# A spectral filter and a SwiGLU block on one core: idle products, a pipeline distance and the places of preparation in the first batch

## The chip, the core and the metric

The kernel runs on one core of a Trainium2 chip. The core has five engines with a queue each: TensorE (PE; its weight loads are listed apart as PEld), VectorE (DVE), ScalarE (ACT), GpSimd (POOL) and SyncE (SP), which in this kernel issues most of the DMAs. The metric is device time in microseconds, from the first to the last instruction of one launch and what lies around them; less is better. The time before is the median of five runs.

## The reference

There are two parts. The first filters x along the sequence in the frequency domain; the second is a SwiGLU block with weights given in float64.

```python
batch, seq, dim = (8, 3008, 256);  d_ff = 1536
X = np.fft.rfft(x, axis=1)
F = (filt_r + 1j * filt_i)[None, :, :]
y = np.fft.irfft(X * F, n=x.shape[1], axis=1).astype(np.float32)
x = y.reshape(B * S, D)                       # 24064 tokens of 256
g = x @ w_gate                                # 256 x 1536
silu = g * (1.0 / (1.0 + np.exp(-g)))
val = x @ w_val                               # 256 x 1536
out = (silu * val @ w_out).astype(np.float32) # 1536 x 256
```

## The kernel before

**The filter** of one batch is a Fourier transform in steps, 3008 = 47 x 64. Stage 1 multiplies x with a small table (`stage1_first` in the first batch, tiles `wpa`; `stage1` later, tiles `pa`). The middle steps, twelve of them (`u` from 0 to 11), are: `turn` (transposes, `wpt`), `stage2a` (a product with a table, `wpb`, then products with the filter on DVE and their sum on POOL) and `stage2b` (the way back, `wpc`, a copy on ACT and a write to the DRAM tile `d`). Stage 3 reads that tile again and makes the filtered y of one chunk of 376 tokens (`wpd` for the first chunk, `pd` for the others). In the first batch all of this up to the first chunk stands at the front of the program, with nothing else to do; in later batches it is spread over the steps of the batch before.

**The SwiGLU block** works through 8 batches x 8 chunks x 3 groups of hidden columns. One such step (class `Group`) is a list of tokens, `SCHEDULE`, that fixes the order of all instructions by hand. Its products with the weights follow a scheme that saves products: 26 products of 128-wide pieces, in order `Q0 Q1 P3 P1 P0 A13 Q2 P2 A01 B13 B01 Q3 A02 A12 E12 B02 E02 B12 E13 A23 A03 E23 E01 B23 E03 B03`. `P` and `Q` take pieces of y (tile `y`, PSUM tile `wk`); `A`, `B` and `E` take sums of pieces (tile `y_t`, PSUM tiles `wa`, `we`) and sums of weights. The weights lie in `wt_t` in that same order, two slots of 128 columns to a product. `D` tokens are differences that POOL makes (tile `D`) before the products of a pair can go on; `S` tokens are sums of the hidden activations on POOL (`h`); `W` and `o` are the projection of the step before (`wA`, `wF`, `wG`, added to `o`); `t` tokens run pieces of the filter; `n` tokens make or reload the sums of the next chunk (`combine_sequence`, `reload_sums`).

**The order in the first batch.** Steps 0 to 8 take chunks 0, 1, 2 in group 0, then in group 1, then in group 2. So y of these chunks is kept in DRAM (`keep_y`) and read again (`reload_y`, L927 of the profile) for the next step; at step 8 it is y of chunk 3, whose sums are made right after. Such extra work hangs on a token of a step by `chore`.

**The weights' rounding.** The float64 weights are rounded on the core (`round_half`: four DVE, four ACT and one or more POOL instructions for each of 36 halves, L302 to L342), and sums of weights are made from them (`combine_weights`: a sum on DVE, for three of the six pairs a factor on ACT, two sums on POOL, L225 to L232). Class `Preparation` puts these on a line of ticks: half `i` begins 4 ticks after the one before, 8 where the first projection half (`i` = 8) begins. A tick issues its instructions in program order, where it stands. There are 8 ticks in stage 1, two in each middle step, and `finish(0)` runs those that the first step needs; after that `TICKS` ticks are spread over a step, and `finish(step)` runs the remaining ones that a step needs at its start.

**Idle products.** `idle(t, banks, n)` issues matmuls whose result nobody reads, one a PSUM bank. There are five at the start, two before the fifth and two before the seventh part of stage 1, 14 on finished weights ahead of stage 3 (`warm`), and three behind it. PE takes its matmuls in order. An fp32 matmul is two passes in the profile, so a count of x4 is two products.

The waits that the build writes into the program are semaphore counts on the writer of what is read. Buffers come from pools that rotate: seven PSUM banks of one pool carry all tiles whose name begins with `w`.

## Time and profile before

| | us |
|---|---|
| median of 5 runs | 2964.26 |
| lowest, highest | 2963.31, 2966.64 |
| the profiled execution's own time | 2966.64 |
| its span, first to last instruction | 2964.9 |
| PE busy | 2925.2 |
| DVE, ACT, POOL busy | 1931.8, 1610.5, 1584.8 |

The mean granted clock of the profiled execution is 0.996. The chain of waits that ended last is PE for 92% of the span, and no other engine has more than 1% of it. How full the engines are in the first batch's parts (busy us in the stretch, and the granted clock of PE):

| stretch, us | what | PE | DVE | ACT | POOL | clock |
|---|---|---|---|---|---|---|
| 8 to 28 | stage 1 | 19.41 | 7.77 | 8.99 | 0.00 | 1.00 |
| 28 to 72 | middle steps | 30.17 | 35.70 | 31.11 | 21.96 | 0.92 |
| 72 to 87 | sums of weights, stage 3 | 14.89 | 10.85 | 7.40 | 12.45 | 0.88 |
| 87 to 120 | step 0 | 26.56 | 25.70 | 23.40 | 24.22 | 0.90 |
| 120 to 200 | steps 1 to 3 | 76.11 | 68.67 | 58.04 | 71.26 | 1.00 |
| 200 to 340 | steps 3 to 7 | 136.40 | 113.05 | 83.37 | 78.29 | 1.00 |
| 340 to 373 | step 8 | 29.77 | 20.96 | 14.71 | 21.87 | 0.95 |

A busy PE in this table counts idle products too. In the lines that follow, the first number is the start from the span's begin, the second the length; in square brackets stands how long the engine had been idle before and what ended it. A line of the weights' or y's sums carries the line number of the helper (`add` L225, `sub` L228, `negated_sum` L232), so its tiles tell which it is.

### The profile page before, as it was taken

How to read it: one execution, taken by the hardware profiler on the slowest of the kernel's cores; microseconds unless marked ns; L12 is line 12 of the kernel's file. 1: busy time of each engine (PE TensorE's matmuls, PEld its weight loads, DVE VectorE, ACT ScalarE, POOL GpSimd, SP SyncE). 2: the span in 40 equal slices, each digit the busy share in tenths (PEclk: the TensorE clock that was granted, in tenths of full speed). 3: DMA queues.
4: the chain of work that ended last, by engine and by line, in shares of the span. 5: the costliest groups of instructions: out<-in, count | busy, mean ns of one | idle time of the engine just before them, and what ended most of it. 6: DMA issues, size and time to landing. Idle time of an engine off the chain costs nothing.

```text
span 2964.9 us, 57673 instructions
## 1 busy us (share of the span) xinstructions
PE 2925.2 (99%) x20292; PEld 2826.5 (95%) x20292; DVE 1931.8 (65%) x4379; ACT 1610.5 (54%) x4207; POOL 1584.8 (53%) x1764
## 2 busy tenths in 40 slices
PE   7999999999999999999999999999999999999999
PEld 5888999999999999999999999999999999999999
DVE  5888765576655766557765577656676566766665
ACT  5775455555555555554555554555555555555554
POOL 3776464455545464446554555544564545555453
PEclk9999999999999999999999999999999999999999
DMA  8577865566555755557555566465665566644442
GB/s 211 184 257 256 275 214 165 186 205 199 174 182 181 219 185 174 189 177 224 188 169 182 186 206 209 153 191 187 198 207 162 185 203 189 208 139 148 147 132 89
DMA packets 217081, 558.59 MB, mean 188 GB/s; under 512 B 29872, under 2 KB 107552, under 8 KB 216512
## 3 DMA queue, kind: packets, MB, share of 16 engines
q1 hardware_dynamic: 170954, 485.59, 52.1%
q10 hardware_dynamic: 36912, 45.43, 4.5%
q0 software_dynamic: 8928, 23.89, 2.3%
q8 instruction: 163, 2.67, 0.4%
q14 instruction: 124, 1.02, 0.1%
HBM read 459.73 MB, written 95.05 MB: 187 GB/s over the span
## 4 chain that ended last, share of the span: by engine, by line
PE 92%; DVE 1%; DMA 1%; POOL 1%; issue 0%; SPq 0%; ACT 0%; ACTq 0%
PE wa L731 24%; PE wA L810 17%; PE wk L731 16%; PE we L731 12%; PE wG L810 8%; PE wF L810 4%; PE pd L639 3%; PE pa L551 3%; PE pc L623 2%; PE pb L591 2%; DMA y<-y 0%; DMA lent<-in_filt_r_dram 0%; DMA lent<-de_tbl 0%; POOL wt_t L225 0%; POOL wt_t L228 0%
## 5 line engine op out<-in xcount | busy, mean ns | idle before, releaser
L731 PE MATMUL wa<-y_t,wt_t 128*128 128x188 f32 x4464 | 882.7, 324 | 9.6 <-DVE wa L753 2.9
L731 PEld LDWEIGHTS wa<-y_t,wt_t 128*128 128x128 f32 x4464 | 732.0, 191 | 35.1 <-issue 14.4
L225 POOL TENSOR_TENSOR h<-h 128x376 f32<-128x376 f32 x190 | 182.8, 983 | 793.9 <-DVE h L778 793.9
L810 PE MATMUL wA<-wo_t,h 128*128 128x128 f32 x4608 | 577.9, 275 | 3.8 <-DVE o L225 3.0
L810 PEld LDWEIGHTS wA<-wo_t,h 128*128 128x128 f32 x4608 | 562.9, 192 | 18.0 <-issue 11.2
L731 PE MATMUL wk<-y,wt_t 128*128 128x188 f32 x2976 | 568.0, 324 | 0.0
L228 POOL TENSOR_TENSOR h<-h 128x376 f32<-128x376 f32 x570 | 555.6, 996 | 0.5
L731 PEld LDWEIGHTS wk<-y,wt_t 128*128 128x128 f32 x2976 | 479.2, 191 | 25.9 <-issue 19.8
L228 DVE TENSOR_TENSOR we<-we,m 128x376 f32<-128x376 f32 x576 | 318.7, 556 | 198.4 <-PE we L731 140.6
L731 PE MATMUL we<-y_t,wt_t 128*128 128x188 f32 x2232 | 432.7, 323 | 0.6 <-ACT we L762 0.5
L731 PEld LDWEIGHTS we<-y_t,wt_t 128*128 128x128 f32 x2232 | 370.6, 190 | 1.4 <-ACT we L762 1.0
L228 POOL TENSOR_TENSOR D<-f,f 128x376 f32<-128x376 f32 x288 | 279.9, 985 | 104.7 <-ACT f L746 103.9
L232 DVE SCALAR_TENSOR_TENSOR y<-wk,c 128x376 f32<-128x376 f32 x480 | 245.1, 543 | 132.3 <-ACT we L762 82.6
L766 ACT COPY m<-wa 128x376 f32<-128x376 f32 x576 | 271.9, 472 | 88.7 <-PE wa L731 87.7
L773 ACT ACTIVATE g<-wa 128x188 f32<-128x188 f32 x576 | 187.9, 326 | 189.2 <-PE wa L731 181.6
L810 PE MATMUL wG<-wo_t,h 128*128 128x128 f32 x2304 | 288.3, 275 | 0.6 <-DVE o L225 0.6
L810 PEld LDWEIGHTS wG<-wo_t,h 128*128 128x128 f32 x2304 | 281.4, 192 | 0.8 <-DVE o L225 0.8
L773 ACT ACTIVATE u<-we 128x188 f32<-128x188 f32 x576 | 188.9, 328 | 167.4 <-DVE we L228 148.3
L746 ACT ACTIVATE f<-wk 128x376 f32<-128x376 f32 x288 | 139.2, 483 | 236.3 <-PE wk L731 213.6
L750 ACT COPY c<-wk 128x376 f32<-128x376 f32 x288 | 136.0, 472 | 226.7 <-PE wk L731 226.7
L753 DVE SCALAR_TENSOR_TENSOR x<-wk,f 128x376 f32<-128x376 f32 x192 | 104.6, 545 | 230.2 <-PE wk L731 228.9
L762 ACT COPY we<-y 128x376 f32<-128x376 f32 x480 | 223.8, 486 | 32.8 <-DVE h L778 14.2
(140 smaller groups left out, 3936.3 us busy)
## 6 DMA issues: line engine op xcount, KB each, us to landing
wt_t<-w_all SPq DMA_DIRECT2D x174, 896.0 KB
wt_t<-w_all SPq DMA_DIRECT2D x174, 768.0 KB
t<-d SPq DMA_DIRECT2D x62, 384.0 KB
d<-t ACTq DMA_DIRECT2D x112, 192.0 KB
lent<-de_tbl SPq DMA_DIRECT2D x84, 256.0 KB
lent<-in_filt_r_dram SPq DMA_DIRECT2D x336, 64.0 KB
lent<-d SPq DMA_DIRECT2D x84, 256.0 KB
d<-lent ACTq DMA_DIRECT2D x84, 256.0 KB
```

Source lines behind the costliest of these rows:

```text
L225: return eng.tensor_tensor(out=dst, in0=a, in1=b, op=ALU.add)
L228: return eng.tensor_tensor(out=dst, in0=a, in1=b, op=ALU.subtract)
L232: return nc.vector.scalar_tensor_tensor(out=dst, in0=a, scalar=-1.0, in1=b, op0=ALU.mult, op1=ALU.subtract)
L551: pin(nc.tensor.matmul(out=ps[0:NK], lhsT=wf_t, rhs=self.x.pop(u), start=True, stop=True))
L731: pin(nc.tensor.matmul(out=ps[:, z], lhsT=self.wt[:, SLOT[p], z], rhs=rhs, start=start and z == 0, stop=True, skip_group_check=True))
L746: pin(act.mul(self.small(f"f{i}", f"f{i}", 1), t[f"k{i}"], -1.0))
L750: pin(act.copy(out=self.small(f"c{i}", f"c{i}", 1), in_=t[f"k{i}"]))
L753: pin(v.scalar_tensor_tensor(out=dst, in0=t[f"k{j}"], scalar=-1.0, in1=t[f"f{i}" if j == 3 else f"D{at}"], op0=ALU.mult, op1=ALU.add))
L762: pin(act.copy(out=self.bank(f"e{at}"), in_=t[f"y{at}"]))
L766: pin(act.copy(out=self.small(f"m{at}", "m", 4), in_=t[f"a{at}"]))
L773: pin(act.activation(out=self.small(op, "g", 3, 1)[:, 0], in_=ps[:, 1], func=AF.Silu))
L810: pin(nc.tensor.matmul(out=self.tiles[at][:, t, :], lhsT=self.hs[i][:, HID[p], t0:t0 + 128], rhs=wo_t[:, JB * q + i, WO[p], :], start=star ...
```

## The change

Only the first batch changes. Stage 1 gets one or two idle products before each part but the first: ten in all, not four. The middle steps run `stage2b` four steps behind `stage2a`, not three. The 14 idle products of `warm` are replaced by eight, in four pairs; a pair reads the slot of a weights' sum (A13, A01, A02, A12) and, as its moving operand of 512 columns, that slot and the next one in the order of products. The first projection half begins 16 ticks after the one before it, not 8, and a step has 22 ticks, not 20. `reload_y` hangs on P0, the fifth product of a step, from step 3 on; at step 2 it stays at A02, the thirteenth.

```diff
@@ class Preparation
-                b = base[-1] + (4 if i != 2 * len(BLOCKS) else 8) if i else 0
+                b = base[-1] + (4 if i != 2 * len(BLOCKS) else 16) if i else 0
...
-    TICKS = 20
+    TICKS = 22
@@ idle products
-    def warm():
-
-        banks = [bank("idle") for _ in range(NB)]
-        for n in (TQ, 2 * TQ):
-            idle(wt_t[:, 0:2].rearrange("p s z f -> p (s z f)"), banks, n)
@@ the front of the first batch
         for u in range(8):
-            if u in (4, 6):
-                idle(zero, [bank("idle") for _ in range(2)], 512)
+            if u:
+                idle(zero, [bank("idle") for _ in range(2 - u % 2)], 512)
             spec.stage1_first(u)
...
-        lag = 3
+        lag = 4
...
         preparation.finish(0)
-        warm()
+        for p in ("A13", "A01", "A02", "A12"):
+            at = SLOT[p]
+            idle(wt_t[:, at:at + 2].rearrange("p s z f -> p (s z f)"),
+                 [bank("idle") for _ in range(2)], 512)
         for step in (0, 2, 1, 3):
             run(spec.stage3(0, step))
@@ chores
     for step in range(NT - 1, NT * NG):
-        chore(step, "A02", lambda s: reload_y(order_of(0)[s + 1][0], s), step)
+        chore(step, "A02" if step < NT else "P0", lambda s: reload_y(order_of(0)[s + 1][0], s), step)
```

## The prediction

> **What bounds the kernel now.** I read the page's busy shares first. TensorE (PE) is busy for 2925.2 of 2964.9 us, so no more than about 40 us can be won without removing products, and a stretch table says where they lie: nearly all before 373 us, in the first batch, which is the part that changes.

> ```profile
> PE 2925.2 (99%) x20292; PEld 2826.5 (95%) x20292; DVE 1931.8 (65%) x4379; ACT 1610.5 (54%) x4207; POOL 1584.8 (53%) x1764
> 28.00:72.00 44.00, 30.17 (x137) 22.47 (x135) 35.70 (x65) 31.11 (x63) 21.96 (x28) 0.92 0.85 212
> 87.00:120.00 33.00, 26.56 (x146) 24.24 (x144) 25.70 (x59) 23.40 (x66) 24.22 (x31) 0.90 0.45 143
> 373.00:2964.90 2591.90, 2585.38 (x18168) 2519.91 (x18166) 1648.49 (x3786) 1382.01 (x3624) 1354.58 (x1471) 1.00 0.57 182
> ```

> The columns after the length are busy us of PE, its weight loads, DVE, ACT, POOL, then granted clock, DMA share, GB/s. From 28 to 72 us (the middle steps) DVE is the fullest engine.

> Next the timeline of PE at the front, and DVE's waits between 29.9 and 72 us.

> ```profile
> 8.75 7.28 PE L564 MATMUL wpa<-wf_t,wo_t 94*128 94x96 f32 x64
> 15.87 1.91 PE L461 MATMUL widle<-room 128*128 128x512 f32 x4
> 17.62 3.71 PE L564 MATMUL wpa<-wf_t,y_t 94*128 94x96 f32 x32
> 27.02 0.33 PE L577 MATMUL wpt<-unit,lent 128*128 128x128 f32 x1 [0.40 <-ACT lent L568]
> DVE room L600 <- ACT y_t L616: 2.8, 5, 0.7
> DVE room L603 <- PE wpb L591: 1.9, 1, 1.9
> DVE w L302 <- POOL wt_t L228: 0.7, 2, 0.4
> ```

> Stage 1 runs on PE without a gap from 8.75 us: it waits for no load. In the middle steps DVE waits for PE once, at the start.

> Last, the timelines of 72 to 98 us and around 359 us.

> ```profile
> 72.11 2.08 PE L623 MATMUL wpc<-room,tb 128*128 128x256 f32 x4 [1.61 <-POOL room L225]
> 73.98 7.58 PE L461 MATMUL widle<-wt_t 128*128 128x188 f32 x28
> 81.40 3.71 PE L639 MATMUL wpd<-wi_t,f 96*128 96x94 f32 x32
> 84.94 2.77 PE L461 MATMUL widle<-room 128*128 128x512 f32 x6
> 84.50 0.77 POOL L225 TENSOR_TENSOR wt_t<-wt_t 128x256 f32<-128x256 f32 x1
> 88.22 0.73 POOL L225 TENSOR_TENSOR wt_t<-wt_t 128x256 f32<-128x256 f32 x1
> 96.41 0.97 POOL L228 TENSOR_TENSOR D<-f,f 128x376 f32<-128x376 f32 x1
> 98.04 1.22 PE L731 MATMUL wa<-y_t,wt_t 128*128 128x188 f32 x6 [2.94 <-DVE wa L753]
> 358.94 0.43 SPq L927 DMA_DIRECT2D y<-y  x1
> 367.46 0.92 ACT L682 ACTIVATE y_t<-y 128x376 f32<-128x376 f32 x2 [3.57 <-DMA y<-y]
> 369.02 1.60 PE L731 MATMUL wa<-y_t,wt_t 128*128 128x188 f32 x4 [2.04 <-ACT wa L757]
> ```

> After the last middle product PE idles on purpose for 7.6 us, then makes y (wpd). POOL has the weights' twelve sums until 88.95, y's sums until 96.4, and only then D01, for which PE stands 2.94 us.

> **1. Ten idle products in stage 1 instead of four: +5.25 us.** Two old ones hold PE from 15.87 to 17.62, so one costs 0.875 us; six more are 6 x 0.875 = 5.25. Nothing hides them. Stage 1 is on PE, the first transpose at 27.02 waits for the copy of its last bank, and DVE's chain starts from the transposes. They could be free only if x landed late, but SP's issue times (an issue is held until the eighth transfer before it has landed) show x in the core 1.2 to 1.7 us before PE wants it, even with the old idle products. Bounds 4.5 and 5.7 (0.955 each with pipeline ends).

> [...] Row: from 7.26 to 33.9 us the clock is at 1.00 throughout, and it fell in windows where PE was busy little, as in 65.29 to 68.70 (1.21 of 3.41 us, no gap over 2.2). So stage 1 has no half clock to win back. [...]

> **2. Distance of four: 0.** PE gets to a wpc one step later and waits less there (its waits on wpc are 9.3 us in all), but DVE's waits in these steps are for ACT's copies L616 and POOL, never for PE after the first. The tail ends, as now, with the sum of step 11 on POOL (72.06) and one wpc. Bounds: -1.0 (this wpc at full clock, 1.10 for 2.08) and +1.1 (one more of ACT's copies with its DMA issue in the tail). I take 0, by DVE's row.

> **3. Idle products by the sums of weights, and later rounding of the projection: +3.0 at D01.** In times of before (add 5.25): the build shows that the last pair reads two slots, A12 and the next one, E12, so it waits for POOL's eighth weight sum. That ends at 85.27 now. Moving the projection's rounding away takes seven DVE instructions of 0.28 to 0.95 (about 5 us beside POOL) and POOL's L329 at 86.83 out of this stretch. POOL's adds then take 0.70 to 0.74, as at 87.53, instead of 0.90 once DVE is done, so E12 comes at 84.7. Six earlier products start at 77.5, when the first sum is there, and cost 0.875 at full and 1.7 at half clock (0.853 a pass before 7.26); they end at 84.5 to 85.9. Two more after E12: 86.4 to 87.7, I take 87.0 where wpd now starts at 81.4. Then wpd 3.7 and the three old idle products 2.6: first group product at 93.3, now 87.55. y is done 1.1 after wpd, at 91.85, now 88.35 (ACT's copy waited for the rounding until 85.87, so 2 us of the later start are given back). y's sums start 0.6 us later on DVE's share of them and need the same 6.9 us of POOL (89.50 to 96.41): D01 starts at 99.4, now 96.41. Bounds: -1.5 (the seven instructions gone, products hidden) and +4.3 (POOL at 0.90, clock half throughout).

> [...] Row: at 98.04 PE stands for 2.94 us at one product while later ones on y alone are ready. [...]

> **4. Step 0 after D01: gives back 1.0.** DVE runs from 97.42 to 120.40 with 3.2 us of idle; 0.9 and 1.07 of these come from PE at half clock (99.42 to 106.25, after the 2.94 us gap). PE now arrives at D01's product at 100.85, when it is ready about 101.1, so that gap and that half clock go; DVE is next and keeps some 20 us of work. Step 0 ends 3.0 - 1.0 = +2.0 late (bounds +0.5, +3.5). The first projection product of step 1 now also waits for L329 of the last rounding, POOL's turn at 122.2 against 120.21: the same 2.0, no more.

> **5. Rounding at 22 a step, from 8 steps later: +0.5.** The same instructions, in fewer steps. DVE is at 69 and POOL at 71 of 80 us between 120 and 200, where PE stands 3.9 us; a tenth more rounding in steps 1 and 2 is about 0.8 us a step on each. Bounds 0 and +2.

> **6. y's reload at P0 from step 3: -3.0.** At step 8 it would be issued near 347, not 358.94, right after the sums' reload; it lands in about 8.4 us, as it does now by the chain of waits, well before 367.46. PE's 2.04 goes, and the half clock from 369.08 to 372.49 with it (1.7): -3.7. What is queued behind it on SP: a part of the weights, one set of table, filters and data (used at 362.55), sums, two reloads of o. It passes 0.77 MB, 2 us at the 407 GB/s of 364 to 368, so that set may be late by 0.7 where now only the one at 350.52 is (1.19). I take -3.0, bounds -3.7 and -0.5. In steps 3 to 7 nobody waits for y. The reload of o, for which PE stood about 2.1 us between 256 and 268, finds another order of raw weights in front of it: -0.3, bounds -2 and +1.

> **Sum:** 5.25 + 0 + 2.0 + 0.5 - 3.0 - 0.3 = +4.4 us. The profiled execution took 2966.64 (span 2964.9 and 1.7 around it); it would take 2971.0. It is 2.4 above the median of the runs, 2964.26, so the median becomes 2968.7. A measurement of this kernel can tell about 0.2% (5.9 us) from no change: my forecast lies within.

> **Rivals.**
> - Slower by over 0.2%: the wait for E12. One mechanism, PE held in order in front of y. If POOL stays at 0.90 and the clock at half, D01 is 4.3 later, and if DVE is too full to give anything back, the sum, with the reload at half its gain, is 5.25 + 4.3 + 0.5 - 1.5 = +8.5: 2972.8. It decides from D01 at 99.9 on (in times of before). [...] Against: DVE idles 3.2 us there. Chance 0.36.
> - The moved reload doesn't help, because its transfer pushes the set behind it: part 6 is 0, +7.4, 2971.7. For it: DMA share 0.98 from 348 to 356. Chance 0.08.
> - Step 0 swallows the front: its PE gaps (2.94, 0.95, 1.41, 1.31) and 2.9 us of half clock are 9.5 us, and if not DVE but those set its end, step 0 gives 5 us back: +0.4, 2964.7. Against: DVE's 3.2 us of idle. Chance 0.12.
> - Faster by over 0.2%: the six products lie in waits for x, and parts 3, 5 and 6 reach their good ends: -1.5 - 3.7 - 2 = -7.2, 2957.1. Against: the gapless rows. Chance 0.06.

> **How the numbers follow.** The forecast has 0.38; with the swallowing case 0.50 within 0.2%, 0.44 slower, 0.06 faster. The forecast's own range is 2966.5 to 2970.0. The range for 8 in 10 runs from 2962.5 (swallowing, o's waits gone, part 5 at 0) to 2974.8 (the E12 case with parts 1 and 5 at their high ends).

> **What would show it.** The first transpose at 32.3; DVE's middle steps as long as now (29.93 to 70.65, moved); an idle pair held by POOL ahead of wpd, wpd near 92; D01 near 104.7 with no PE gap of 2.9 before it and no half clock after; no wait for y near 370. A first transpose before 30, or wpd before 88, breaks parts 1 or 3; a wait for a set at step 8 of over 2 us breaks part 6.

## The result, and the profile after

| | before | after |
|---|---|---|
| median, us | 2965.06 (42 runs) | 2970.73 (22 runs) |
| the profiled execution | 2966.64 | 2970.13 |
| its span | 2964.9 | 2968.3 |

The ratio is 1.0021, with a 95% interval from 1.0015 to 1.0027: 6.2 us by the ratio, 5.7 by the medians, 3.5 between the two profiled executions. The forecast was +4.4 us and 2968.7; the range, 2962.5 to 2974.8, holds the time, which is 0.7 above the top of the forecast's own range (2966.5 to 2970.0). The change is slower by just about the 0.2% that the prediction drew as the bound, so "within 0.2%" and "slower by over 0.2%" can't be told apart: the interval lies on both sides.

(One description above is to be corrected: a chunk has 752 tokens, in two halves of 376, so there are 8 batches x 4 chunks x 3 groups = 96 steps of about 31 us. No number of the prediction rests on it.)

The page's busy shares of the kernel after, then two rows of the stretch table for each kernel (busy us of PE, its weight loads, DVE, ACT, POOL; granted clock, DMA share, GB/s). The first two rows are steps 1 and 2, from ACT's first copy `f` of step 1 to that of step 3, before and after; the last two are step 8, before and after:

```profile
PE 2928.6 (99%) x20292; PEld 2824.5 (95%) x20292; DVE 1925.8 (65%) x4379; ACT 1612.1 (54%) x4207; POOL 1584.4 (53%) x1764
119.95:187.65 67.70, 63.76 (x444) 60.12 (x445) 58.94 (x125) 48.80 (x136) 59.49 (x78) 1.00 0.66 216
126.90:196.88 69.98, 65.57 (x444) 62.81 (x443) 58.56 (x128) 50.37 (x140) 60.84 (x82) 0.95 0.62 202
342.06:377.73 35.67, 32.44 (x211) 31.47 (x210) 22.16 (x48) 15.79 (x42) 24.79 (x27) 0.95 0.83 285
350.18:381.18 31.00, 30.52 (x211) 29.69 (x210) 21.92 (x48) 15.62 (x41) 23.58 (x26) 1.00 0.87 296
```

Step 8 takes 31.00 us where it took 35.67, at a clock of 1.00 for 0.95: the moved reload. Steps 1 and 2 are the other way round, 69.98 for 67.70 and 0.95 for 1.00. That loss of 2.3 us is more than the 0.5 that the forecast had for the rounding there.

PE's timeline at the end of stage 1, and one row of DVE's waits in the middle steps (34.65 to 75.36 us):

```profile
31.37 0.33 PE L571 MATMUL wpt<-unit,lent 128*128 128x128 f32 x1
32.26 1.42 PE L571 MATMUL wpt<-unit,lent 128*128 128x128 f32 x11 [0.56 <-DVE lent L562]
DVE room L594 <- ACT y_t L610: 2.8, 5, 0.7
```

The transposes come 4.35 and 4.72 us later than in the kernel before. DVE's wait for ACT is the same to the last digit, and its stretch is 40.71 us against 40.72.

The timeline of PE and one of its weight loads (PEld) around stage 3, then POOL's:

```profile
76.82 2.08 PE L617 MATMUL wpc<-room,tb 128*128 128x256 f32 x4 [2.44 <-POOL room L225]
82.06 9.36 PE L461 MATMUL widle<-wt_t 128*128 128x512 f32 x16 [3.16 <-POOL wt_t L341]
89.30 0.43 PEld L461 LDWEIGHTS widle<-wt_t 128*128 128x128 f32 x2 [0.43 <-POOL wt_t L225]
91.25 3.71 PE L633 MATMUL wpd<-wi_t,f 96*128 96x94 f32 x32
105.20 1.54 PE L725 MATMUL wa<-y_t,wt_t 128*128 128x188 f32 x8 [0.29 <-DVE wa L747]
```

```profile
88.53 0.72 POOL L225 TENSOR_TENSOR wt_t<-wt_t 128x256 f32<-128x256 f32 x1
96.79 2.29 POOL L225 TENSOR_TENSOR y_t<-y_t 128x376 f32<-128x376 f32 x2 [4.81 <-DVE y_t L225]
103.57 2.88 POOL L228 TENSOR_TENSOR D<-f,f 128x376 f32<-128x376 f32 x3
```

wpd starts at 91.25 (forecast near 92), D01 at 103.57 (near 104.7). POOL now stands 4.81 us for y, and PE's wait of 2.94 ahead of `wa` is 0.29. E12 is the sum that ends at 89.25. A weight load of the last pair waited for it (89.30), but the pair's first pass starts at 89.54, without a gap of PE: E12 came just in time. What holds the pairs is their start at 82.06 and five passes at half clock (0.50 until 86.60). The row names L341, the rounding that writes Q2, as what the start waits for: the first pair reads Q2 as the slot beside A13. A13 itself is made by DVE and ACT (its factor on ACT ends at 81.96), so none of POOL's twelve sums is in that wait.

PE's timeline in steps 0 to 2, and in step 8:

```profile
126.54 1.60 PE L804 MATMUL wF<-wo_t,h 128*128 128x128 f32 x10 [2.58 <-POOL wo_t L329]
180.01 0.90 PE L725 MATMUL wa<-y_t,wt_t 128*128 128x188 f32 x4 [1.59 <-ACT m L760]
185.70 1.62 PE L725 MATMUL we<-y_t,wt_t 128*128 128x188 f32 x4 [1.46 <-DVE we L232]
357.92 1.10 PE L585 MATMUL pb<-lent 128*128 128x256 f32 x4 [0.48 <-DMA lent<-d]
374.26 0.80 PE L725 MATMUL wa<-y_t,wt_t 128*128 128x188 f32 x4
```

The last row stands where the wait of 2.04 us was. How much later each mark comes (for a step, ACT's first copy `f` of it):

| mark | before | after | later by |
|---|---|---|---|
| last wpc | 72.11 | 76.82 | 4.71 |
| D01 | 96.41 | 103.57 | 7.16 |
| step 1 | 119.95 | 126.90 | 6.95 |
| step 2 | 151.87 | 158.64 | 6.77 |
| step 3 | 187.65 | 196.88 | 9.23 |
| step 5 | 248.19 | 258.38 | 10.19 |
| step 8 | 342.06 | 350.18 | 8.12 |
| step 12 | 466.87 | 470.33 | 3.45 |
| end | 2964.86 | 2968.34 | 3.49 |

### The profile page after: what moved, and what is told of

It reads as the page before. It is cut to its first block, busy times and chain, and to the rows that moved or that the text cites. A ratio compares the mean times of both kernels' runs of the same rounds, so it can differ in the third digit from the quotient of the medians.

```text
span 2968.3 us, 57673 instructions
## 1 busy us (share of the span) xinstructions
PE 2928.6 (99%) x20292; PEld 2824.5 (95%) x20292; DVE 1925.8 (65%) x4379; ACT 1612.1 (54%) x4207; POOL 1584.4 (53%) x1764
## 4 chain that ended last, share of the span: by engine, by line
PE 93%; DVE 1%; POOL 1%; DMA 1%; issue 0%; ACT 0%; SPq 0%; ACTq 0%; POOLq 0%
PE wa L725 24%; PE wA L804 17%; PE wk L725 16%; PE we L725 12%; PE wG L804 8%; PE wF L804 4%; PE pd L633 3%; PE pa L545 3%; PE pc L617 2%; PE pb L585 2%; POOL y_t L225 0%; DMA d<-lent 0%; DMA lent<-de_tbl 0%; DMA lent<-d 0%; POOL D L228 0%
## 5 line engine op out<-in xcount | busy, mean ns | idle before, releaser
L225 POOL TENSOR_TENSOR h<-h 128x376 f32<-128x376 f32 x190 | 183.1, 985 | 779.9 <-DVE h L772 770.3
L228 POOL TENSOR_TENSOR h<-h 128x376 f32<-128x376 f32 x570 | 555.4, 995 | 0.5
L228 DVE TENSOR_TENSOR we<-we,m 128x376 f32<-128x376 f32 x576 | 318.9, 556 | 196.4 <-PE we L725 139.8
L228 POOL TENSOR_TENSOR D<-f,f 128x376 f32<-128x376 f32 x288 | 280.5, 987 | 104.4 <-ACT f L740 103.8
```

Of the source, the lines that this page charges most:

```text
L225: return eng.tensor_tensor(out=dst, in0=a, in1=b, op=ALU.add)
L228: return eng.tensor_tensor(out=dst, in0=a, in1=b, op=ALU.subtract)
```

## The experiments

Each kernel stood beside the kernel before on the same chip; the table after the last one has all times with their intervals. An interval is about 2.6 us to each side, so what the medians say of single microseconds is read together with the shifts in the traces.

**Stage 1: four idle products in the kernel after, and none at all.**

```diff
-            if u:
-                idle(zero, [bank("idle") for _ in range(2 - u % 2)], 512)
+            if u in (4, 6):
+                idle(zero, [bank("idle") for _ in range(2)], 512)
```

> The kernel after, with the four idle products of stage 1 as before instead of ten. Theory (the six idle products lie on the path, and nothing later gives their time back): the first transpose comes 4.4 to 5.3 us earlier than after's 31.37, D01 about 4.7 earlier than its 103.57, and the time falls by 4.7 us from after's, to about 2966.0. Rival (the front is swallowed later, as the swallowing case had it): the transposes come earlier but step 0 or the waits for the rounding in steps 1 to 3 give it back, and the time falls by less than 1.5 us. A second rival (fewer idle products let the clock fall in stage 1): the first transpose comes less than 3 us earlier, with a granted clock under 1.00 between 8 and 30 us.

The first transpose came at 26.60, D01 at 98.45, 5.12 earlier than in the kernel after, and steps 1, 2 and 3 are 5.14 earlier each (step 3 at +4.09 instead of +9.23 against before). The median is 2965.52, 5.2 below the kernel after. The six products cost their full length and nothing gives it back. The theory holds.

```diff
 # the kernel before, with y reloaded at P0 from step 3 on
-            if u in (4, 6):
-                idle(zero, [bank("idle") for _ in range(2)], 512)
```

> The kernel before with y reloaded at P0 from step 3 on, and stage 1 without any idle product. Theory (stage 1 waits for no load and keeps its clock, so an idle product there costs its 0.87 us and nothing hides it): the first transpose comes 3.5 us earlier than with four, near 23, the granted clock stays at 1.00 from the first full window to the transposes, and the time falls by 3.5 us from the 2961.6 that the moved reload alone gave, to about 2958. Rival (the idle products filled waits for x that show without them): PE waits for x between 9 and 20 us, the first transpose comes less than 1.5 us earlier, the clock falls once in stage 1 or just behind it, and the time stays at 2960.5 or more.

PE's timeline and one row of the stretch table of this kernel:

```profile
15.79 3.78 PE L564 MATMUL wpa<-wf_t,y_t 94*128 94x96 f32 x32 [0.56 <-DMA y_t<-in_x_dram]
20.68 5.29 PE L564 MATMUL wpa<-wf_t,x 94*128 94x96 f32 x32 [1.11 <-DMA x<-in_x_dram]
19.28:22.69 3.41, 2.30 (x21) 2.16 (x21) 0.83 (x1) 2.31 (x5) 0.00 (x0) 1.00 1.06 261
```

Now PE does wait for x, at both places where two idle products had stood, and behind the second wait the clock is at half from 22.69 to 32.93. The first transpose comes at 25.76, 0.56 us earlier than with four, but D01 comes at 97.67 for 95.68. The median is 2963.88, 2.2 above the kernel with four, which was measured on another chip; its runs spread from 2959.55 to 2966.45. By the ratios to the kernel before the two are the same (0.9992 and 0.9993), so no loss of time is shown, only that the expected 3.5 us were not there to win. The rival's mechanism holds: the first four filled 1.7 us of waits and kept the clock, and the next six had nothing left to fill. That fits the prediction's row: with four, PE wanted these parts of x at 17.62 and 22.91, 1.8 and 2.2 us later than the two waits end here (the prediction had 1.2 to 1.7).

**The distance of the middle steps: three in the kernel after.**

```diff
-        lag = 4
+        lag = 3
```

> The kernel after, with the middle steps' distance of three as before. Theory (DVE carries these steps and the distance moves nothing): DVE's stretch from its first product to its last stays at 40.7 us, the last wpc starts near 76.8, and the time stays within 1 us of after's 2970.6. Rival (the longer distance keeps PE fuller and so warmer, or adds one more of ACT's copies to the tail): the last wpc moves by over 1 us in one direction and the time by as much.

2970.54, as after. The last wpc starts at 75.93 instead of 76.82, but the first transpose of this execution, which lies ahead of the edit, was already 0.87 earlier (30.50), so the middle steps are as long as after's. D01 is 0.45 and steps 3 to 8 are 0.28 earlier; the end of this profiled execution is 0.9 later. No effect that can be measured, as the theory has it.

**The idle products ahead of stage 3.** First the 14 as before, then the eight of the change, but on finished weights:

```diff
-        for p in ("A13", "A01", "A02", "A12"):
-            at = SLOT[p]
-            idle(wt_t[:, at:at + 2]..., [bank("idle") for _ in range(2)], 512)
+        banks = [bank("idle") for _ in range(NB)]
+        for n in (TQ, 2 * TQ):
+            idle(wt_t[:, 0:2].rearrange("p s z f -> p (s z f)"), banks, n)
```

> The kernel after, with the 14 idle products on finished weights ahead of stage 3 as before, in place of the four pairs on the sums of weights. Theory (the pairs hold PE in order in front of y): wpd starts near 86.3 instead of 91.25; POOL ends the weights' sums at 92 as now and goes on to y's sums at once, so D01 comes near 98.8 instead of 103.57, 4.8 earlier; PE then stands about 2 us for D01 as it did before, and the time falls by about 3 us. Rival (the step after sets the end, the wait is only moved): D01 comes earlier, but the waits for the rounding at step 1's first projection product and in step 2 take it up, and the time changes by less than 1 us.

```diff
         for p in ("A13", "A01", "A02", "A12"):
-            at = SLOT[p]
+            at = 0
```

> The kernel after, with the same eight idle products of 512 columns, but all of them on the finished weights of the first slots, so none waits for a sum of weights. Theory (what holds wpd is that the first pair waits 3.16 us for POOL; the products themselves fit into the 9.2 us that y's last piece takes from its write to its reload): the pairs follow the last wpc at once, wpd starts within 0.5 us of 86.4, where it waits for the reload, D01 comes near 98.8, and the time falls by 3.3 us, as with the 14 shorter products. Rival (eight long products at half clock are themselves too long): wpd comes at 87.5 or later and the time falls by less than 2.5 us.

PE's timeline of the first, then of the second:

```profile
86.40 3.78 PE L633 MATMUL wpd<-wi_t,f 96*128 96x94 f32 x32 [1.43 <-DMA f<-d]
```

```profile
78.05 8.00 PE L461 MATMUL widle<-wt_t 128*128 128x512 f32 x16
85.89 3.71 PE L633 MATMUL wpd<-wi_t,f 96*128 96x94 f32 x32
```

D01 came at 98.80 and 98.73 (98.8 expected), step 1 was 4.78 and 4.85 us earlier than in the kernel after, and the medians are 2967.30 and 2966.89: 3.4 and 3.8 below it. Both theories hold in their times; of the details, PE stands 0.29 us for D01 in the first kernel and not 2, and in the second wpd follows the pairs without a wait.

With the 14 products wpd waits 1.43 us for the reload of the tile `d`, 9.2 us after the last wpc started: here they lie in the shadow of that round trip. The eight on finished weights end 9.7 us after it, so they are about as long. With the eight of the change wpd comes 14.43 us after it. Of the 4.7 us more, 3.4 are the later start of the pairs, which is their wait for POOL, and 1.4 are more passes at half clock. In the kernel before, wpd came 9.29 us after the last wpc with no wait ahead of it. SP began the last reads of `d` earlier there (77.44, 5.3 us after the last wpc, for 6.6 with the 14 above), so its idle products may have reached past the reload; no run tests this.

**The rounding: begin and density, each alone and together.** Both as before:

```diff
-                b = base[-1] + (4 if i != 2 * len(BLOCKS) else 16) if i else 0
+                b = base[-1] + (4 if i != 2 * len(BLOCKS) else 8) if i else 0
-    TICKS = 22
+    TICKS = 20
```

> The kernel after, with the projection's first half 8 ticks behind the one before it and 20 ticks a step, as before. Theory (part 5 was set too low; the later and denser rounding costs 2.3 us in steps 1 to 3, where PE stood 2.58 us for the last rounding ahead of step 1's projection and 4.0 us between 180 and 186): these gaps go, D01 comes 0.5 to 1.5 us later because the rounding stands in front of it again, and the time falls by about 1.5 us. Rival (the move of the rounding earns more at the front than it costs later): D01 comes 2 to 3 us later and the time rises by 1 us or more.

2970.25, 0.5 below the kernel after. D01 came at 103.78, 0.2 later. But the last wpc took 1.13 us here, at full clock, and 2.08 in the kernel after; the next kernel, whose front is that of the kernel after, has it at full clock too and D01 at 102.97. So the rounding's move out of the front wins 0.2 to 0.8 us at D01 while the pairs hold y. On POOL it wins more: the weights' sums end 14.21 us after the last wpc in the next kernel, for 15.85 here. The gaps of steps 1 to 3 went as expected: step 3 is at +6.49 against before, instead of +9.23. But the kernel after makes up 2.9 us in step 5 and this one doesn't, so little is left of it. Neither theory foresaw that.

Only the density as before (`TICKS = 20`, first projection half still 16 ticks behind):

> The kernel after, with 20 ticks a step as before, but the projection's first half 16 ticks behind. It tells which half of part 5 makes the loss of steps 1 to 3 (a wait of 2.58 us ahead of step 1's projection, gaps of 4 us between 180 and 186 and half clock behind each). Theory (the later begin makes the first wait, the denser ticks the second): the wait near 126.5 stays at 2.5 us or more, the gaps between 180 and 186 shrink to about 2.4 us as with both edits undone, and the shift at step 3 is about 7.5 against after's 9.23. Rival (the later begin makes both): both stay, and the shift at step 3 is 9 or more.

```profile
127.27 2.50 PE L804 MATMUL wF<-wo_t,h 128*128 128x128 f32 x10 [4.05 <-POOL wo_t L329]
```

This row of PE's timeline shows the first wait grown to 4.05 us. Between 180 and 190 there are 1.8 us of gaps and no half clock; step 3 is at +8.24. So the later begin makes the first wait; the shift lies between the theory's 7.5 and the rival's 9. The median is 2969.74, 1.0 below the kernel after, which the runs don't tell from nothing.

Only the begin as before (8 ticks behind, `TICKS = 22`):

> The kernel after with the projection's first half 8 ticks behind, as before, and 22 ticks a step, as after. So far: with 20 ticks and 8 the kernel after took 2970.25, with 20 and 16 2969.74, with 22 and 16 2970.6; in the kernel before with the moved reload, 22 ticks instead of 20 earned 2.1 us. Theory (the denser ticks earn about 2 us wherever the rounding begins early, and the later begin takes that away again): the wait ahead of step 1's projection falls from 2.58 us to 1.5 or less, the gaps of 4 us between 180 and 186 shrink under 3.5 with no half clock behind them, and the time falls by 2 us or more, to 2968.6 or less. Rival (what the denser ticks earn hangs on the kernel before's front, not on the begin): the time stays within 1 us of 2970.6.

```profile
126.51 1.35 PE L804 MATMUL wF<-wo_t,h 128*128 128x128 f32 x10 [0.96 <-DVE h L772]
177.89 0.90 PE L725 MATMUL wa<-y_t,wt_t 128*128 128x188 f32 x4 [1.24 <-ACT wa L751]
```

In this timeline of PE the wait for the last rounding is gone. Where the gaps of 180 to 186 were, now near 178, 1.24 us are left and no half clock behind them; step 3 is at +5.94. The median is 2967.88, 2.9 below the kernel after (the profiled execution, with a half clock in step 6, is among its slower ones). The theory holds in this row: with 22 ticks the later begin costs some 2.9 us, and with the early begin the denser ticks earn 2.4. But with 20 ticks the later begin cost nothing (2969.74 against 2970.25), so what one edit does hangs on the other, and the two can't simply be added.

Where the denser ticks earn it, the stretch table shows for the same work, from the second copy `f` of step 5 to its third subtraction `we`; the first row is the kernel before, the second the kernel after:

```profile
252.00:272.60 20.60, 18.52 (x119) 16.40 (x118) 16.22 (x37) 12.06 (x34) 18.38 (x24) 1.00 0.63 209
```

```profile
262.34:280.06 17.72, 17.72 (x121) 16.70 (x120) 14.53 (x35) 12.05 (x34) 13.80 (x18) 1.00 0.77 251
```

The stretch is 2.9 us shorter. PE had 2.1 us of gaps there and has none, and it counts as busy for 0.8 less. POOL is no longer nearly full. Before, eight sums of weights of the last group stood on POOL in this stretch, among step 5's differences `D`, and DVE waited 2.9 us for one of these (1.4 after). With 22 ticks a step only two of the sums are left in it.

**The reload of y: alone, and taken out of the change.**

```diff
 # the kernel before
-        chore(step, "A02", lambda s: reload_y(order_of(0)[s + 1][0], s), step)
+        chore(step, "A02" if step < NT else "P0", lambda s: reload_y(order_of(0)[s + 1][0], s), step)
```

> The kernel before, with one part of the change alone: y is reloaded at P0 from step 3 on. Theory (the wait for y and the half clock that follows it are lost time, and nothing else is pushed back): no PE gap near 369 and no half clock after it, steps up to 8 as before, and the time falls by 3.7 to 4.5 us from before's. The prediction had 3.0, as one set for the filter was to come 0.7 late; then the PE gap at 350.5 would grow from 1.19 to about 1.9. Rival (the wait is only handed on to that set): the gap at 350.5 grows to over 3 us and the time falls by less than 1 us.

PE's timeline of step 8:

```profile
351.90 1.51 PE L731 MATMUL wa<-y_t,wt_t 128*128 128x188 f32 x8 [0.79 <-DMA y_t<-yt]
361.96 1.10 PE L591 MATMUL pb<-lent 128*128 128x256 f32 x4 [0.54 <-DMA lent<-d]
```

The wait near 369 and its half clock are gone, and from step 8 to step 12 the kernel gains 3.05 us (its shift against before goes from -1.61 to -4.66; the first 1.6 are other half clocks of this execution, in the front). It is under the expected 3.7 because a wait for the sums' reload, 0.79, is new, and the set that the prediction had 0.7 late is 0.54 late; the set before it, whose wait was 1.19 and was expected to grow, waits 0.33. The median is 2961.64, 2.7 below before (2.1 by the ratio, whose interval just reaches 1). This is the prediction's 3.0, with the set late as it said and the sums as a latecomer that it did not have.

The other way round, the kernel after with the reload back at A02:

> The kernel after, with y reloaded at A02 in all steps as before. In the kernel before the same move alone earned 2.7 us by the medians and 3.05 by the shift of steps 8 to 12, with 0.79 and 0.54 of new waits for sets and sums; in the kernel after the shift over these steps is 4.0 to 4.7. Theory (the moves of the rounding have cleared SP's queue around step 8, so the reload is worth its full 3.7 to 4.7 here): the wait near 374 comes back with about 2 us and half clock behind it, and the time rises by 3.7 to 4.7, to about 2974.8. Rival (its worth is the same, and the rest of the shift belongs to the rounding): the time rises by 2.5 to 3.2 us.

2974.63 in six runs, 3.9 above the kernel after by the medians. The wait came back (1.52 us near 377), but in the profiled execution no half clock followed it, and the shift from step 8 to 12 differs by only 1.8 us from the kernel after. Theory and rival are 1 us apart, and this does not decide between them.

```diff
 # the kernel before with the moved reload
-    TICKS = 20
+    TICKS = 22
```

> The kernel before with y reloaded at P0 from step 3 on and 22 ticks a step, the projection's first half 8 ticks behind as before. With both moves undone the reload was worth 2.7 us, and 4.0 in the kernel after. Theory (with denser ticks the raw weights have left SP's queue earlier, so the sets of step 8 come in time): the shift from step 8 to step 12 against before is 4 us or more, instead of 3.05; the denser ticks cost 1 to 1.5 us in step 2, and the time is within 1 us of 2961.6. Rival (the extra worth belongs to the later begin, not to the density): the shift stays near 3.05, and the time rises by 1 us or more, to 2962.6 or later.

2959.53, 2.1 below the moved reload alone and 5.2 below before (ratio 0.9983, interval 0.9974 to 0.9992). It beats both kernels. From step 8 to step 12 it gains 3.72 us, between theory and rival. The kernel with 20 ticks and no idle product in stage 1 is the same program over these steps as the moved reload alone, and gains 4.41 there instead of 3.05, so this mark can't tell the two apart. What I had wrong in both is the sign: the denser ticks cost nothing in step 2 here and earn 2.9 us in the stretch of step 5 shown above (17.72 for 20.60).

One more pair of ticks, 24:

> The kernel before with y reloaded at P0 from step 3 on and 24 ticks a step; 20 took 2961.64, 22 took 2959.53. Theory (denser ticks end the rounding earlier in each step, so that fewer of its pieces stand between a step's own instructions late in steps 1, 2 and 5, and raw weights leave SP's queue earlier): the gaps between 155 and 200 us, 2.8 us of waits over 0.25 with 20 ticks, change little, the stretch from step 5 on is no longer than with 22, and the time falls by a further 0.5 to 2 us. Rival (DVE and POOL are near full in steps 1 to 3, and more ticks crowd them): the time rises by 1 us or more, with PE gaps for ACT and DVE over 5 us in all between 120 and 200.

2962.68, 3.2 above 22 ticks. PE's gaps over 0.3 us between 120 and 200 sum to 5.3; the longest, 2.34 us for DVE at 164.55, has half clock behind it. The rival holds: step 2 is crowded now and takes 38.68 us, for 35.22 with 22 ticks. Of the theory, the later steps are right: from step 3 to step 8 it takes 151.46 us, for 153.24.

| kernel | median, us | before beside it | ratio | 95% interval |
|---|---|---|---|---|
| after | 2970.73 | 2965.06 | 1.0021 | 1.0015 to 1.0027 |
| after, four in stage 1 | 2965.52 | 2964.34 | 1.0004 | 0.9995 to 1.0012 |
| after, 14 products on finished weights | 2967.30 | 2964.34 | 1.0010 | 1.0001 to 1.0019 |
| after, pairs on finished weights | 2966.89 | 2964.85 | 1.0010 | 1.0001 to 1.0019 |
| after, distance of three | 2970.54 | 2964.85 | 1.0019 | 1.0010 to 1.0028 |
| after, 8 and 20 ticks | 2970.25 | 2964.34 | 1.0020 | 1.0011 to 1.0029 |
| after, 16 and 20 ticks | 2969.74 | 2964.85 | 1.0017 | 1.0008 to 1.0025 |
| after, 8 and 22 ticks | 2967.88 | 2964.60 | 1.0012 | 1.0003 to 1.0021 |
| after, reload at A02 | 2974.63 | 2964.85 | 1.0032 | 1.0020 to 1.0043 |
| before, reload at P0 | 2961.64 | 2964.34 | 0.9993 | 0.9984 to 1.0001 |
| the same, no idle in stage 1 | 2963.88 | 2964.77 | 0.9992 | 0.9983 to 1.0001 |
| before, P0 and 22 ticks | 2959.53 | 2964.77 | 0.9983 | 0.9974 to 0.9992 |
| before, P0 and 24 ticks | 2962.68 | 2964.60 | 0.9993 | 0.9984 to 1.0002 |

## Why the prediction came near, and where it was wrong

By the ratios, undoing one part of the kernel after at a time (a ratio of 0.0001 is 0.3 us) gives stage 1 5.0, the distance 0.6, the pairs 3.2, the rounding 0.3, the reload -3.3; they add up to 5.8 of the 6.2 us. Each is a difference of two measurements and known to some 3 us. The sum came near because its largest terms, the first and the reload, are right; the 2.0 of parts 3 and 4 is nearer 3, and 0.5 for the rounding is luck.

- **Part 1, +5.25: right.** 5.0 by the ratios, 5.2 by the medians, 5.12 at D01.
- **Part 2, 0: right**, by DVE's row as argued: 40.71 us for 40.72.
- **Part 3, +3.0 at D01: right in kind and nearly in size.** D01 moved by 7.16 - 4.71 = 2.45. The start of the pairs (5.4 us behind the last wpc by the prediction, 5.24 measured) and wpd fit. The 2.45 is made of two terms. D01 comes 24.30 us after the last wpc in the kernel before, 22.54 with the pairs on finished weights and 26.75 in the kernel after, each with that wpc at half clock. So the move of the rounding earns about 1.8 as long as nothing holds y, since POOL is through with the weights' sums 1.6 earlier (15.20 for 16.84), and the pairs cost 4.2, under which that gain is hidden. The rival's mechanism, PE held for E12, hardly happened: E12 came 0.29 us ahead of its product, and in the kernel with the reload back at A02, whose front is the same, PE stood 0.33 us for it.
- **Part 4, "gives back 1.0": wrong, and the first step that failed.** D01 is 7.16 late and step 1 still 6.95. The gap of 2.94 and its half clock did go, but at the first projection product "the same 2.0, no more" was 2.58 us of wait and a half clock behind it (0.50 from 127.56 to 130.97). The rounding that had been taken from the front stood there. The wait is 2.58 too with the pairs on finished weights, where D01 is 4.84 earlier, so it hangs on the place of the rounding and not on D01. Whether step 0 would have given time back with the rounding as before is not shown: with both rounding edits undone it takes 90.36 us from D01 to step 3, and the program of the kernel before took 91.24 in its own execution and 90.35 in that with the moved reload, which differs only later.
- **Part 5, +0.5: right by accident.** The net is 0.3 to 0.5. Undone apart, the edits do not add: the medians are 2970.25 (first projection half 8 ticks behind, 20 ticks a step), 2969.74 (16, 20), 2967.88 (8, 22) and 2970.73 (16, 22). Each difference is no larger than its uncertainty of some 3 us, but from D01 to step 3 the traces take 90.36, 92.92, 89.70 and 93.31 us: the later begin costs 2.6 to 3.6 us there. The step that failed is the reading "a tenth more rounding ... is about 0.8 us a step on each": it counted instructions in a stretch, and what decides is which of them stand in front of a needed one, L329 in step 1 and the sums of weights in step 5.
- **Part 6, -3.0: right in kind, at most 1 too small** (-3.3 by the ratio, -3.9 by the medians; -2.1 and -2.7 alone in the kernel before). In the kernel after the set that was to be 0.7 late came in time, and the wait for the one before it fell from 1.19 to 0.48; alone in the kernel before it was 0.54 late. The sum's further -0.3 laid PE's gaps between 256 and 268 to the reload of o. They went with the denser ticks, in a stretch where DVE waited for POOL, and belong to part 5.

Of the rivals, "step 0 swallows the front" is refuted by D01 and step 1 (7.16 and 6.95) and by the six idle products alone, which move D01 by 5.12 and steps 1, 2 and 3 by 5.14 each. "The reload doesn't help" is refuted by step 8 (31.00 us for 35.67) and by the kernel with the reload back at A02. "Faster" had the six products lie in waits for x: only the old four do.

On "stage 1 has no half clock to win back": with ten idle products the clock is at 1.00 there throughout (7.5 to 31.4 us), as the prediction read it for four. With none it fell behind a window with 1.11 us of idle time (19.28 to 22.69). So the kernel without the old four lost clock there (0.50 from 22.69 to 32.93), and the six new ones had none to win.

## What to carry to other kernels

An idle product pays only while it fills a wait; count the waits first, then add no more products than they hold, and let none of them wait for something that is later than the work behind it. Rounding or other preparation that is moved out of a crowded place is not gone: follow each piece to the place where it is next needed, and test its begin and its density apart and together, since what one of them does can hang on the other. A gain ahead of a wait does not show while the wait is there: here the earlier sums of weights showed only once the pairs no longer held PE. And a short gap on PE had two prices here: the wait of 2.04 us at step 8 of the kernel before had 3.41 us of half clock behind it, the wait of 1.52 us in the kernel with the reload back at A02 had none. So compare many runs, or the shifts between marks, rather than the ends of two profiles.

## What the runs showed of the hardware

The granted clock of PE is 1.00 or 0.50 in the traces of the kernels before and after. Rows of the stretch table around three of its drops, the first three rows from the kernel before, the last four from the kernel after:

```profile
96.01:99.42 3.41, 1.38 (x8) 1.25 (x8) 2.00 (x6) 0.75 (x3) 3.41 (x5) 1.00 0.96 312
99.42:102.84 3.42, 2.46 (x10) 2.31 (x10) 3.42 (x7) 2.72 (x9) 3.21 (x6) 0.50 1.07 341
102.84:106.25 3.41, 3.41 (x14) 3.41 (x14) 2.52 (x9) 2.42 (x5) 0.00 (x0) 0.50 0.06 14
124.15:127.56 3.41, 1.02 (x9) 1.02 (x10) 3.41 (x8) 2.07 (x6) 3.33 (x5) 1.00 0.84 333
127.56:130.97 3.41, 3.41 (x17) 3.41 (x16) 0.74 (x2) 1.16 (x3) 3.41 (x7) 0.50 0.67 236
182.18:185.59 3.41, 1.14 (x7) 0.69 (x5) 2.86 (x6) 2.76 (x9) 3.29 (x5) 1.00 0.64 257
185.59:189.00 3.41, 3.30 (x11) 3.30 (x12) 3.41 (x11) 1.77 (x5) 3.41 (x6) 0.50 0.08 9
```

At 0.50 the four `wa` passes at 369.02 in the kernel before take 1.60 us, for 0.80 at 1.00 (374.26 in the kernel after). So the wait of 2.04 us ahead of them cost an estimated further 1.7 us, half of the 3.41 us of half clock behind it. The length of a wait alone does not tell whether this happens: behind a wait of 1.96 us, at 60.35 in the kernel before, the clock stayed at 1.00.

In stage 1 without idle products the clock fell behind a stretch in which PE was busy for 2.30 of 3.41 us (19.28 to 22.69), and was still at half behind one in which it was busy throughout (22.69 to 26.11). Why these two differ from the others, no run here tests.
